# Loading the second stage's input two units at a time, with two tiles' space given up for it

## The chip, the core and the metric

The kernel runs on one core of a Trainium2 chip. The core has five engines that the text names as the profile does: PE (TensorE, matmuls; PEld is its weight load), DVE (VectorE), ACT (ScalarE), POOL (GpSimd) and SP (SyncE, which here only issues DMAs). The DMAs run on 16 DMA engines. The metric is the device time of one execution in microseconds (us); less is better.

## What is computed

All data are float32. First a causal convolution along the sequence, written in the reference with Fourier transforms, for 8 batches of 5696 positions and 128 channels; then a soft mixture of experts over all 45568 tokens.

```python
def _attn_ref(x, h):                      # x (8, 5696, 128), h (5696, 128)
    L = 2 * S
    Yf = np.fft.rfft(x, n=L, axis=1) * np.fft.rfft(h, n=L, axis=0)[None]
    return np.fft.irfft(Yf, n=L, axis=1)[:, :S, :]

def _moe_ref(x, phi, w1, w2):             # x (45568, 128), phi (128, 32), 8 experts of 4 slots, F = 1024
    logits = x @ phi
    d = softmax(logits, axis=0)           # over tokens
    slot_input = (d.T @ x).reshape(E, S_per_e, D)
    for e in range(E):
        slot_out[e] = np.maximum(slot_input[e] @ w1[e], 0.0) @ w2[e]
    c = softmax(logits, axis=1)           # over slots
    return c @ slot_out.reshape(n_slots, D)
```

## The kernel before

The transform is split into two steps of lengths 90 and 64, made of matmuls with cosine and sine tables. There are nine groups of work: group 0 is the filter h, groups 1 to 8 are the batches of x.

**First stage** (`load_x`, `fold`, `stage_a`; words `loadx`, `fold`, `low`, `high` in the order below). POOL adds and subtracts mirrored rows (line 216), PE multiplies by the first table (line 240), ACT copies the result from PSUM into a tile `fst` (line 242), and SP stores it to DRAM: `fl` for the lower half of the frequencies, `fh` for the rest (line 224 issues what was put off until the word `flush`).

**Second stage** (`load_g`, `stage_b1`, `stage_b2`; words `loadf`, `forward`, `backward`). A group has 12 units, numbered through from 0 to 107. `load_g` (line 274) brings one unit's input back from `fl` or `fh` into a tile `gt` of 4 KB in each of 128 partitions, in three buffers; the last unit of a group has 1 KB. `stage_b1` multiplies it (line 287, tile `bt`), and DVE multiplies the result by the filter's spectrum (lines 306 and 313); for group 0 DVE makes the spectrum itself (`Hr`, `Hi`, line 310). `stage_b2` transforms back (line 328, tile `bz`), ACT copies to `zst` (line 333), and after every second unit SP stores to DRAM: `zm`, or `zr` for the last rows.

**Third stage**, in 32 tiles T of 8 rows x 2 halves, four a batch. `load_main` and `load_rest` bring `zc` and `zx`; `stage_c1` (word `product`) multiplies them (lines 419 and 424) and begins to add and subtract halves into one of two tiles `y`, whose slots are addressed by `part(v, f)`; `after` (word `sums`) finishes: DVE makes the odd sum `op` and difference `om` (lines 411 and 412), POOL adds and subtracts them into y's slots (line 437). `part` transposes y (line 447), `logits` multiplies by phi into `lt`, `maximum` keeps a running column maximum, `exponents` (words `expd`, `exponent`; line 496) writes the exponentials `dt`, `stage_c5` (word `tokens`, line 505) transposes them and copies them to a tile `d` (line 508), from which `dispatch` (line 546) sums tokens into slots. Other words are the softmax over slots (`turnl`, `shift`, `exp`, `rowsum`, `scale`, `weights`).

**The order** is written out by hand: `run` takes a text of words and calls the stage that each names, with its number. Every engine carries out its instructions in this order, so a DMA whose buffer isn't free holds up all that SP is to issue after it. A loop of four passes covers batches 1 to 4 in the third stage. From `front.close()` on, the tiles of the first two stages are gone and a pool `last` stands in their place; `tail` is then filled, and `stage_c1` has DVE do part of POOL's sums. The last part is the experts and the product with `c`, line 883 and after.

Of the kernel before, what the change touches and what calls it, by code (L numbers as in the profile page):

```python
# [12 lines left out]
F32 = mybir.dt.float32  # L13
# [62 lines left out]
def kernel(  # L76
# [25 lines left out]
    P = 128  # L102
# [155 lines left out]
    def parts(u):  # L258

        g, w = divmod(u, NW)  # L260
        return g, w, [(i, min(2, NP - 2 * i)) for i in range(2 * w, min(2 * w + 2, NU))]

    def load_g(u):
        if u >= (B + 1) * NW:
            return
        g, w, us = parts(u)
        n = sum(k for _, k in us)
        t_ = bpool.tile([P, 4, 2, D], F32, name="gt", tag="gt", bufs=3)
        if 8 * w < LOW:
            src = fl[g].rearrange("h a n l o k x -> (a n l o) h (k x)")  # L270
        else:
            src = fh[g].rearrange("h a n l c o k x -> (a n l c o) h (k x)")
        k0 = 4 * w % (LOW // 2) * 2 * D
        nc.sync.dma_start(
            out=t_[:, 0:n, :, :].rearrange("p q c d -> p (q c d)"), in_=src[:, :, k0:k0 + n * 2 * D])
        gs[u] = t_
# [83 lines left out]
    om, op = [ypool.tile([P, CH, D], F32, name=n) for n in ("om", "op")]  # L360
    yt = ypool.tile([D, Q * CH, 2, MH], F32, name="yt")
    nc.vector.memset(rests[0][:, :, :, :, :], 0.0)
    for t_ in (lt, dt):
        nc.vector.memset(t_[:, :, :, :], 0.0)
    nc.vector.memset(lt[HP:P, :, :, MH - 1:MH], -2.0 ** 127)
# [35 lines left out]
    def stage_c1(T, between=lambda: None):  # L401
        zt, zx = zs.pop(T), rest.pop(T)[:, T % 2]
        y_ = ybufs.pop(0)
        ybufs.append(y_)

        def part(v, f):
            k = (2 * v + f) * CH
            return y_[:, k:k + CH, 0:D] if f == 0 else y_[:, k + CH - 1:k - 1:-1, 0:D]

        def fold_out(even, minus, plus):  # L410
            nc.vector.tensor_tensor(out=plus, in0=even, in1=minus, op=AL.add)  # L411
            nc.vector.tensor_tensor(out=minus, in0=even, in1=minus, op=AL.subtract)

        ps = {(o, c): bank() for o, c in ((0, 1), (1, 0), (0, 0), (1, 1))}
        for c in (1, 0):
            for h_ in range(2):
                for o in range(2):
                    r = slice(o * HP, (o + 1) * HP)
                    nc.tensor.matmul(ps[o, c][h_ * HP:(h_ + 1) * HP, :], im[r, c, :],  # L419
                                     zt[r, h_, :, c, :], start=True, stop=False)  # L420
        for h_ in range(2):
            for (o, c), p in ps.items():
                r = slice((2 * o + c) * HALF, (2 * o + c) * HALF + N1 - MAIN)
                nc.tensor.matmul(p[h_ * HP:(h_ + 1) * HP, :], ir[r, :], zx[r, h_, :, :],  # L424
                                 start=False, stop=True)
        ps = {k: p[:, :].rearrange("p (n d) -> p n d", d=D) for k, p in ps.items()}
        nc.scalar.activation(part(0, 0), ps[0, 1], AF.Copy)  # L427
        nc.scalar.activation(om[:, :, :], ps[1, 0], AF.Copy)
        fold_out(ps[0, 0], part(0, 0), part(1, 0))
        a_ = ps[1, 1]  # L430
        between()

        def after():
            fold_out(a_, om[:, :, :], op[:, :, :])
            for v, o_, eng in ((1, op, nc.gpsimd), (0, om, nc.vector if tail else nc.gpsimd)):
                for part_, sign in ((part(v, 1), AL.subtract), (part(v, 0), AL.add)):
                    eng.tensor_tensor(out=part_, in0=part(v, 0), in1=o_[:, :, :], op=sign)  # L437

        ys[T] = y_
        return after  # L440
# [53 lines left out]
    def exponents(T):  # L494
        for r, m in ((slice(0, P), slice(0, MH - 1)), (slice(0, HP), slice(MH - 1, MH))):
            nc.scalar.activation(dt[r, :, :, m], lt[r, :, :, m], AF.Exp,
                                 bias=low[r, T % 2:T % 2 + 1])
        if T:
            e_ = cpool.tile([P, 1], F32, name="dn", tag="dn")
            nc.scalar.activation(e_[:, :], lows.pop(T)[:, :], AF.Exp)  # L500
            scales[T] = e_
    def stage_c5(T):
# [4 lines left out]
        d_ = ypool.tile([P, CH, P], F32, name="d", tag="d", bufs=1)  # L507
        nc.scalar.activation(d_[:, :, :].rearrange("p i s -> p (i s)"), p[:, :], AF.Copy)
        ds[T] = d_
# [133 lines left out]
    def run(words, batch=0):  # L643
# [29 lines left out]
    for g in range(4):  # L673
        run(
# [54 lines left out]
    tail["last"] = last  # L729
    zring.insert(0, last.tile([P, 2, CH, 2, D], F32, name="zd"))  # L730
# [205 lines left out]
```

## Time and profile before

| | |
|---|---|
| median of 3 runs | 808.36 us (806.04 to 810.59) |
| profiled execution, own time | 805.76 us |
| profiled execution, span from first to last instruction | 803.7 us |
| mean granted TensorE clock | 0.951 |
| PE busy in the span | 712.9 us (89%) |
| DVE busy | 629.3 us (78%) |
| ACT busy | 429.3 us (53%) |
| POOL busy | 410.4 us (51%) |
| packets of SP's queue, share of 16 DMA engines' span | 96.1% |
| moved by DMA | 282.50 MB, 352 GB/s |
| loads of `gt` | 99 of 512 KB and 9 of 128 KB |

Busy time is the union of an engine's instructions. The DMA share adds up the times of packets, which can overlap, so it can be a little over 1. The span leaves out what lies before the first and after the last instruction.

### The profile page before, as it was taken

Reading aid. Unit: us, or ns where it says so; the run is one execution under the profiler, and the core shown is the slowest. Engines: PE = TensorE matmul, PEld = TensorE weight load, DVE = VectorE, ACT = ScalarE, POOL = GpSimd, SP = SyncE. Lnnn points to the kernel's source line nnn. Section 1 sums busy time; section 2 is a strip of 40 time slices with the busy share of each in tenths; the row PEclk is TensorE's granted clock in tenths of the full one; section 3 lists DMA queues with packets and bytes.
Section 4 is the critical chain, followed back from the end, with each engine's and each line's share of the span. In section 5 each row is a group of like instructions: output and inputs, shape, how many; then the busy total and the mean of one; then the engine's idle time right before and its main releaser. Section 6 shows DMA issues by size and latency. Waiting matters only on the chain.

```text
span 803.7 us, 21826 instructions
## 1 busy us (share of the span) xinstructions
PE 712.9 (89%) x8884; PEld 360.5 (45%) x8884; DVE 629.3 (78%) x895; ACT 429.3 (53%) x868; POOL 410.4 (51%) x368
## 2 busy tenths in 40 slices
PE   5768789779999999999999999999998887888882
PEld 1122233324544444554455455444444444356782
DVE  1019988648989999998999999999989996795552
ACT  2334245335666665666666566666565455474441
POOL 5545443425556666656666655566434533686000
PEclk9889999979999999999999999999999998999865
DMA  8999999999999999999999999999999899843998
GB/s 274 357 308 405 332 391 388 330 361 388 389 351 379 383 388 344 397 393 380 361 394 394 355 386 389 399 355 357 374 309 342 282 363 317 317 179 129 385 401 337
DMA packets 164779, 282.50 MB, mean 352 GB/s; under 512 B 9448, under 2 KB 128872, under 8 KB 158440
## 3 DMA queue, kind: packets, MB, share of 16 engines
q1 hardware_dynamic: 163672, 280.01, 96.1%
q8 instruction: 71, 1.16, 0.5%
q10 hardware_dynamic: 1008, 1.10, 0.4%
q14 instruction: 28, 0.23, 0.1%
HBM read 148.54 MB, written 132.53 MB: 350 GB/s over the span
## 4 chain that ended last, share of the span: by engine, by line
PE 62%; DVE 15%; DMA 14%; ACT 4%; issue 2%; POOL 1%; SPq 1%; ACTq 0%; DVEq 0%; POOLq 0%
PE bank L240 18%; PE bt L287 10%; PE bz L328 8%; PE bank L419 7%; DMA out_dram<-o 4%; PE bank L424 4%; PE bank L447 4%; DMA fl<-fst 4%; DVE yf L306 3%; DVE bt L306 3%; PE bank L456 3%; PE bank L546 2%; DVE yf L313 2%; PE bank L570 2%; DMA gt<-fh 2%
## 5 line engine op out<-in xcount | busy, mean ns | idle before, releaser
L216 POOL TENSOR_TENSOR x<-xc 128x512 f32<-128x512 f32 x144 | 179.1, 1276 | 81.5 <-PE bank L240 53.5
L240 PE MATMUL bank<-x,s 128*32 128x512 f32 x1728 | 207.1, 608 | 14.0 <-POOL x L216 8.1
L242 ACT ACTIVATE fst<-bank 128x512 f32<-128x512 f32 x216 | 125.6, 595 | 84.5 <-PE bank L240 63.3
L287 PE MATMUL bt<-gt,wt 64*64 64x256 f32 x1620 | 117.6, 399 | 26.2 <-DMA gt<-fl 9.7
L333 ACT ACTIVATE zst<-bz 128x1024 f32<-128x1024 f32 x96 | 93.0, 968 | 80.6 <-PE bz L328 74.3
L437 POOL TENSOR_TENSOR y<-y,op 128x512 f32<-128x512 f32 x64 | 78.3, 1223 | 105.2 <-DVE op L411 102.7
L306 DVE TENSOR_TENSOR yf<-bt,Hi 128x1024 f32<-128x1024 f32 x96 | 112.4, 1171 | 16.2 <-PE bt L287 16.1
L313 DVE TENSOR_TENSOR yf<-bt,yf 128x512 f32<-128x512 f32 x192 | 119.3, 663 | 3.3
L306 DVE TENSOR_TENSOR bt<-bt,Hr 128x1024 f32<-128x1024 f32 x96 | 113.0, 1177 | 0.0
L240 PEld LDWEIGHTS bank<-x,s 128*32 128x32 f32 x1728 | 52.2, 111 | 131.8 <-issue 91.8
L328 PE MATMUL bz<-yf,vt 64*64 64x256 f32 x1440 | 100.6, 387 | 4.6 <-DVE yf L313 4.2
L287 PEld LDWEIGHTS bt<-gt,wt 64*64 64x64 f32 x1620 | 54.9, 135 | 87.9 <-issue 35.6
L533 POOL TENSOR_TENSOR L<-L,rs 128x512 f32<-128x512 f32 x32 | 33.6, 1051 | 109.3 <-DVE rs L528 89.5
L328 PEld LDWEIGHTS bz<-yf,vt 64*64 64x64 f32 x1440 | 55.7, 136 | 39.8 <-DVE yf L313 11.8
L437 POOL TENSOR_TENSOR y<-y,om 128x512 f32<-128x512 f32 x54 | 64.1, 1187 | 2.1
L427 ACT ACTIVATE y<-bank 128x512 f32<-128x512 f32 x32 | 19.1, 597 | 81.6 <-PE bank L424 81.6
L447 PE MATMUL bank<-ident,y 109*128 109x109 f32 x512 | 59.4, 261 | 3.1 <-DVE y L437 1.0
L419 PE MATMUL bank<-zc,im 64*64 64x512 f32 x480 | 60.3, 600 | 0.0
L447 PEld LDWEIGHTS bank<-ident,y 109*128 109x128 f32 x512 | 49.7, 141 | 12.7 <-issue 7.9
L306 DVE TENSOR_TENSOR yf<-bt,turn 128x1024 f32<-128x1024 f32 (+1 forms) x12 | 14.0, 1170 | 52.4 <-PE bt L287 52.4
L449 ACT ACTIVATE yt<-bank 128x360 f32<-128x360 f32 x128 | 52.6, 475 | 3.7 <-PE bank L447 3.5
L883 PE MATMUL op<-so,cT 32*128 32x128 f32 x704 | 43.6, 357 | 6.5 <-ACT o L891 6.0
(99 smaller groups left out, 854.9 us busy)
## 6 DMA issues: line engine op xcount, KB each, us to landing
fl<-fst SPq DMA_DIRECT2D x72, 512.0 KB, 7.7
gt<-fl SPq DMA_DIRECT2D x72, 512.0 KB, 7.2
zm<-zst SPq DMA_DIRECT2D x64, 512.0 KB, 9.3
zc<-zm SPq DMA_DIRECT2D x30, 1024.0 KB, 9.1
fh<-fst SPq DMA_DIRECT2D x36, 512.0 KB, 6.6
xc<-in_x_dram SPq DMA_DIRECT2D x32, 512.0 KB, 8.8
out_dram<-o SPq DMA_DIRECT2D x16, 1024.0 KB, 11.2
gt<-fh SPq DMA_DIRECT2D x27, 512.0 KB, 8.2
```

Source lines behind the costliest of these rows:

```text
L216: nc.gpsimd.tensor_tensor(out=y_[:, o, :, :], in0=near, in1=far, op=AL.subtract if o else AL.add)
L240: nc.tensor.matmul(p[i * m:(i + 1) * m, :], s1[:, q + o, cols], columns(c_, o), start=True, stop=True)
L242: nc.scalar.activation(st[:, :, q, :], p[:, :].rearrange("p (n d) -> p n d", d=D), AF.Copy)
L287: nc.tensor.matmul(bt[q * HP:(q + 1) * HP, a, o, :], wt[r, 2 * i + q, :], t_[r, 2 * o + q, :, :].rearrange("p c d -> p (c d)"), start=True ...
L306: nc.vector.tensor_tensor(out=p_, in0=pv, in1=h_, op=AL.mult)
L313: nc.vector.tensor_tensor(out=y_[r, 0:k, c, :], in0=pv[:, :, c, :], in1=y_[r, 0:k, c, :], op=op_)
L328: nc.tensor.matmul(bz[a * HP:(a + 1) * HP, q, o, :], vt[r, i, a, :], y_[r, a * m + o, :, :].rearrange("p c d -> p (c d)"), start=True, sto ...
L333: nc.scalar.activation(zst[:, e_, 0:m, 0:n, :].rearrange("p o q x -> p q o x"), bz[:, 0:n, 0:m, :], AF.Copy)
L419: nc.tensor.matmul(ps[o, c][h_ * HP:(h_ + 1) * HP, :], im[r, c, :], zt[r, h_, :, c, :], start=True, stop=False)
L437: eng.tensor_tensor(out=part_, in0=part(v, 0), in1=o_[:, :, :], op=sign)
L447: nc.tensor.transpose(p[:, i * TR:(i + 1) * TR], ys[T][0:TR, k * CH + i, 0:D], ident[0:TR, 0:TR])
L449: nc.scalar.activation(yt[:, k * CH:(k + 1) * CH, :, :], of_tokens(p), AF.Copy)
```

## The change

Three edits. `load_g` now loads units u and u+1 in one DMA, into a tile of 8 KB in each partition, in two buffers; each unit gets its half, and the words `loadf` with odd numbers are taken out of the order (54 loads instead of 108; those with even numbers stay where they were, but that the first `loadf` words, 0, 1 and 2, become 0 and 2). Outside the tail the odd sum `op` has no tile of its own: it is written to y's slot `part(0, 1)`, which the last but one of POOL's four sums overwrites. `stage_c5` copies the transposed exponentials back into `dt`, from where `dispatch` reads them, instead of a tile `d`; `exponents` now runs over the whole tile in one activation, as `lt` is filled with a large negative number at the start where no token lies. In the tail, `op` and `d` are tiles of the pool `last`. The tiles given up, 4 KB in a partition, are what the larger `gt` takes.

```diff
@@ load_g
-        n = sum(k for _, k in us)
-        t_ = bpool.tile([P, 4, 2, D], F32, name="gt", tag="gt", bufs=3)
+        n = sum(k for _, k in us + parts(u + 1)[2])
+        t_ = bpool.tile([P, 8, 2, D], F32, name="gt", tag="gt", bufs=2)
...
-        gs[u] = t_
+        gs[u], gs[u + 1] = t_[:, 0:4], t_[:, 4:8]
@@ tiles of the third stage
-    om, op = [ypool.tile([P, CH, D], F32, name=n) for n in ("om", "op")]
+    om = ypool.tile([P, CH, D], F32, name="om")
...
-    for t_ in (lt, dt):
-        nc.vector.memset(t_[:, :, :, :], 0.0)
-    nc.vector.memset(lt[HP:P, :, :, MH - 1:MH], -2.0 ** 127)
+    nc.vector.memset(lt[:, :, :, :], -2.0 ** 127)
@@ stage_c1
         def after():
-            fold_out(a_, om[:, :, :], op[:, :, :])
-            for v, o_, eng in ((1, op, nc.gpsimd), (0, om, nc.vector if tail else nc.gpsimd)):
+            op = tail["op"][:, :, :] if tail else part(0, 1)
+            fold_out(a_, om[:, :, :], op)
+            for v, o_, eng in ((1, op, nc.gpsimd), (0, om[:, :, :], nc.vector if tail else nc.gpsimd)):
                 for part_, sign in ((part(v, 1), AL.subtract), (part(v, 0), AL.add)):
-                    eng.tensor_tensor(out=part_, in0=part(v, 0), in1=o_[:, :, :], op=sign)
+                    eng.tensor_tensor(out=part_, in0=part(v, 0), in1=o_, op=sign)
@@ exponents
-        for r, m in ((slice(0, P), slice(0, MH - 1)), (slice(0, HP), slice(MH - 1, MH))):
-            nc.scalar.activation(dt[r, :, :, m], lt[r, :, :, m], AF.Exp,
-                                 bias=low[r, T % 2:T % 2 + 1])
+        nc.scalar.activation(dt[:, :, :, :], lt[:, :, :, :], AF.Exp, bias=low[:, T % 2:T % 2 + 1])
@@ stage_c5
-        d_ = ypool.tile([P, CH, P], F32, name="d", tag="d", bufs=1)
-        nc.scalar.activation(d_[:, :, :].rearrange("p i s -> p (i s)"), p[:, :], AF.Copy)
-        ds[T] = d_
+        d_ = (tail.get("d") or dt)[:, :, :, :].rearrange("p i h r -> p (i h r)")
+        nc.scalar.activation(d_, p[:, :], AF.Copy)
+        ds[T] = d_.rearrange("p (i s) -> p i s", i=CH)
@@ the order, every odd loadf taken out; its first place and one of the loop
-        "loadx5 flush low7 fold8 fold9 flush high7 flush low8 loadf0 loadf1 loadf2 loadx6 flush "
+        "loadx5 flush low7 fold8 fold9 flush high7 flush low8 loadf0 loadf2 loadx6 flush "
...
-            "dispatch0 part5 part6 part7 loadf34 forward32 loadf35 flush backward31 logits1 fold32 "
+            "dispatch0 part5 part6 part7 loadf34 forward32 flush backward31 logits1 fold32 "
@@ after front.close()
+    tail["op"] = last.tile([P, CH, D], F32, name="op")
+    tail["d"] = last.tile([P, CH, 2, HP], F32, name="d")
```

68 rows, old and new, of tables (strides, w1s) are left out of this document.

## The prediction

> **What bounds the kernel now.** I read the page's engine totals, then the busy time by stage, then the chain of waits where an engine idles, then the DMA queue's own waits. By stage (PE, PEld, DVE, ACT, POOL busy with instruction counts, granted clock, DMA share, GB/s):
>
> ```profile
> 49.00:60.00 11.00, 6.93 (x64) 2.37 (x68) 3.65 (x4) 2.28 (x4) 3.36 (x4) 0.69 0.89 287
> 60.00:97.00 37.00, 29.06 (x325) 10.33 (x321) 36.25 (x42) 13.03 (x22) 19.01 (x16) 1.00 0.99 367
> 97.00:144.00 47.00, 40.42 (x510) 16.17 (x503) 39.51 (x46) 23.31 (x32) 19.62 (x16) 1.00 1.05 387
> 148.00:172.00 24.00, 15.60 (x164) 6.53 (x164) 10.95 (x12) 7.16 (x11) 4.98 (x4) 0.87 1.04 359
> 212.00:511.00 299.00, 298.69 (x3810) 148.33 (x3808) 276.63 (x385) 190.82 (x385) 187.98 (x160) 1.00 1.04 379
> 511.00:570.00 59.00, 58.93 (x738) 28.88 (x736) 54.45 (x76) 38.56 (x80) 37.49 (x32) 1.00 1.03 366
> 628.00:636.00 8.00, 6.82 (x84) 3.04 (x88) 7.79 (x15) 4.35 (x12) 1.05 (x1) 1.00 0.53 198
> 636.00:660.00 24.00, 19.81 (x264) 11.34 (x264) 22.93 (x34) 12.42 (x25) 12.53 (x11) 0.94 1.02 363
> ```
>
> From 212 to 570 us PE idles 0.4 us of 358: nothing that shortens a load, the SP queue, ACT or DVE can shorten that stretch; the change can only lengthen it. From 60 to 97 DVE is the bound (36.25 of 37). The DMA engines are as full (shares about 1): they run level with PE. Loads are on the path in three places, in the chain of waits (start, us, what):
>
> ```profile
> 42.57 6.47 DMA fl<-fst
> 49.10 3.92 DMA gt<-fl
> 53.07 1.99 PE bt L287 x16
> ...
> 144.59 4.21 DMA gt<-fl
> ...
> 159.04 7.23 DMA zr<-zst
> 166.35 5.06 DMA zx<-zr
> 171.46 2.01 PE bank L424 x16
> ...
> 636.41 7.18 DMA zm<-zst
> 644.29 12.33 DMA gt<-fh
> 656.76 1.66 PE bt L287 x16
> ```
>
> These are units 0, 24 and 106. Of other units' loads PE waits little, as issues run 10 to 18 us ahead of use (unit 36: 217.81 to 228.78; unit 38: 221.93 to 239.49) and land after a median of 7.8 us.
>
> **The change part by part.** The sum is made on the profiled execution (span 803.7, own time 805.76; the median is 808.36, 2.6 more).
>
> *The first load.* Unit 0's 4 KB rows become 8 KB rows with unit 1. Each of 16 engines moves 8 rows of the 128. The trace's packet records give a median of 159 ns for 4096 bytes and 309 for 8192, so 1.27 us becomes 2.47: forward0 starts 1.2 us later. PE runs forward0 before high9, low10 and forward1, and the DVE chain that fills 60 to 97 hangs on forward1, so all of that shifts by 1.2.
>
> *To 171 us.* From 92 to 144 the DMA engines never run dry (share 1.04), and unit 24's load waits for a store (fl of low23) behind that backlog. The start of this stretch is low15's store, 1.2 later; within it the six pairs save two packets of 159 for one of 309, 8 to an engine: about 0.07 us a pair, 0.4 in all. So loadf24 is issued 0.8 later and, being doubled, lands 2.0 later. But PE had 5.8 us of idle before L424 at 171.46, so forward24 to forward26 may all be late by 2. L424 waits for the chain zr stores, zx load. In SP's order those stores lose one load ahead of them (unit 27's, issued 155.57, 1.32 us), but its bytes are still ahead of them, now in 26's pair, and the queue is full (148 to 172: 1.04). I take 0.75 later at 171.46; bounds -1.9 (the SP time of units 25 and 27, 0.58 and 1.32, counts in full) and +2.0 (nothing absorbed).
>
> *212 to 570.* Even units' loads stand at the same places of SP's order, wait for the same forward, and carry 1.24 us more (0.5 MB at 424 GB/s, sixteen times 8192 bytes in 309 ns); odd units come earlier. The tightest is the first of a group: unit 48, issued 293.21, landed 299.26 by the trace's records, used 303.53: slack 4.3, then 3. The other tight one is zx at the turn of a batch:
>
> ```profile
> PEld bank L424 <- DMA zx<-zr: 3.3, 4, 0.9
> ```
>
> That is weight load idle (us, times, longest) in 212 to 511; PE's matmuls there still run back to back. Unit 39's load, 233.69, goes ahead of zx's, 236.97, today too, so the bytes ahead of zx don't grow. I cost this stretch at 0, bounds -0.4 (all of PE's idle) and +6 (the slower rival).
>
> *SP.* 54 fewer issues at 0.55 us, and fewer waits at L274, which hold every store behind them:
>
> ```profile
> SPq L274 <- PE bt L287: 65.3, 36, 4.3
> ```
>
> In the PE-bound stretch that is free. At the end of the loads it is not: unit 105's load is issued at 639.98 into a queue that is full until 660, while from 628 to 636 the share is 0.53. As 104's pair it goes at 629.29 into that hole, and everything behind it is served some 1.24 us earlier; 106 brings 107's 128 KB along (8 rows an engine, 5 KB for 4: 0.3). Unit 106's wait in the chain ends 0.95 earlier. Bounds 0 and -3 (of the 4.33 us that its issue took). With PE waiting 1.79 there, the next to be late is ACT's copy of the transposed exponentials, L508, 656.43 to 657.0, and dispatch25 behind it.
>
> *op and d.* The DVE sum writes y instead of op; the row that writes y already takes as long. POOL reads y where it read op (1223 ns, against 1187 for om); its idle, 132 us of the 358 from 212 to 570, hides any change: bounds -0.1 and +0.1 us each, in the tail nothing, where op has its own tile. The copy of d into dt makes the next exponents wait for dispatch: 220 against 229.9 in the first batch, ten us of room; queued behind on ACT would be zst and fst copies. If that cover went, ACT would wait out what is missing of it, once a tile. Two exponent activations become one:
>
> ```profile
> L521 ACT ACTIVATE L<-L 128x512 f32<-128x512 f32 x32 | 20.2, 632 | 49.5 <-POOL L L515 49.5
> L496 ACT ACTIVATE dt<-lt,low 128x352 f32<-128x352 f32 x32 | 18.7, 584 | 3.2 <-DVE low L470 3.1
> L496 ACT ACTIVATE dt<-lt,low 64x8 f32<-64x8 f32 x32 | 9.6, 299 | 0.0
> L411 DVE TENSOR_TENSOR op<-bank,om 128x512 f32<-128x512 f32 x32 | 21.8, 680 | 0.0
> L412 DVE TENSOR_TENSOR y<-bank,y 128x512 f32<-128x512 f32 x32 | 22.1, 691 | 1.1
> ```
>
> The pair spans 0.78 us in the timeline, one full tile 0.63: 0.15 saved, on the path two or three times after 570: -0.35. The dropped memsets (0.5 us of DVE at 3.6 us, when it idles) count nothing.
>
> Sum: +0.75 - 0.95 - 0.35 = -0.55: 805.2 for a profiled run, 807.8 as a median. A measurement of this kernel tells about 0.5% (4 us) from no change: I forecast no change.
>
> **The rivals.** *Slower, zx late.* At the turn of a batch 38's load, now 1 MB, goes ahead of the eight zr stores (223.91 to 233.6), and zx's load has to wait until they land. If the 1.24 us isn't returned by the missing load of unit 39, L424 for tiles 4, 8, 12, 16, 20 starts 1.24 late, 6.2 us in five batches. It decides as soon as zx lands over some 0.3 us later than today, as L424 at 245.71 follows L419 without a gap: 807.8 + 6.2 = 814. Against: the bytes ahead are the same.
>
> *Faster, SP was the bound.* If the stores behind L274 gain their issue times in full (-1.9 at 171 and -3 at 656, with 0.35 on ACT), with unit 0's 1.2 us hidden behind them: -5.2, 803.1. Against: in both places the DMA engines are full, and an earlier issue into a full queue lands no earlier.
>
> *Fewer DMAs, fixed cost saved.* Unit 0's load took 3.92 us for 1.27 us of packets. If the other 2.65 us used up the queue, each merged load would give it back, until PE's idle is gone: 6.6 us in 97 to 144, 8.4 in 148 to 172, about 10 in 570 to 660, and the time would be near 785. Against: with 2.65 us idle per load, shares of 1.04 could not be. The Trainium skill (DMA: Bandwidth & Descriptors, Rules for kernel authors) asks for at least 1 MiB per DMA for bandwidth, and its fit of about 2.0 us fixed plus bytes over 436 GB/s would, by an estimate, save 2 us for each of 54 loads; the trace disagrees with that as a cost of throughput, and shows it only as latency.
>
> *Nothing changes.* A pair's buffer comes free only after its second unit, and three buffers were ahead far enough: 808.4.
>
> **How the numbers follow.** Forecast 0.58 (own range 803 to 810: the bounds at 171 and 656), nothing changes 0.06, zx late 0.20, SP the bound 0.13, fixed cost 0.03. Within 0.5% (804.3 to 812.4) are the first two: 0.64. Slower 0.20, faster 0.16. The range runs from SP's case, 803.1 less half a us, to zx late, 814, and half a us: 802.5 to 814.5.
>
> **What would show it.** Right: forward0 at about 54.3, DVE's chain 1.2 late at 61.6, L424 near 172, PE idle still under 1 us between 212 and 570, forward106 about 1 us earlier against forward100, one L496 of some 630 ns a tile. Wrong: PE idle before L424 at each turn of a batch (zx late); zr stores landing 2 us sooner with the DMA share below 1 (SP the bound); a DMA share well below 1.04 in mid-kernel (fixed cost).

## The result: 0.7% slower, 812.0 us against 806.7

The changed kernel takes 811.98 us (median of 10 runs, 807.72 to 818.2), the kernel before 806.72 in the same series (804.12 to 810.59): a ratio of 1.0069, 95% interval 1.0040 to 1.0098. Two later series of the unchanged edit gave 1.0063 (1.0039 to 1.0087) and 1.0094 (1.0067 to 1.0122). The ratios and their intervals are those of the record, which leaves disturbed runs out; they are not just the quotient of two medians. The forecast of no change was wrong; the loss is that of the rival "zx late" in place and nearly in size, though its reason for the lateness did not hold as it was given.

The profiled execution took 808.70 us, with a span of 806.9 (before 805.76 and 803.7). The busy time by stage, in the stretches of the prediction (length, then PE, PEld, DVE, ACT, POOL busy with counts, granted clock, DMA share, GB/s):

```profile
49.00:60.00 11.00, 5.87 (x48) 1.79 (x48) 3.65 (x4) 2.21 (x4) 2.82 (x3) 0.69 0.90 314
148.00:172.00 24.00, 16.50 (x172) 6.21 (x164) 12.10 (x15) 8.20 (x12) 4.98 (x4) 0.93 1.02 353
212.00:511.00 299.00, 296.47 (x3776) 147.36 (x3768) 273.78 (x382) 189.86 (x367) 186.71 (x159) 1.00 1.04 377
511.00:570.00 59.00, 57.39 (x728) 27.66 (x724) 52.43 (x75) 35.31 (x69) 36.43 (x32) 1.00 1.01 350
628.00:636.00 8.00, 6.87 (x108) 4.42 (x106) 7.86 (x14) 2.98 (x6) 4.06 (x4) 1.00 0.95 369
636.00:660.00 24.00, 20.17 (x280) 10.69 (x276) 23.00 (x37) 12.86 (x26) 8.73 (x8) 1.00 0.92 322
```

From 212 to 570 us PE was busy but for 0.4 us; now it idles 2.53 + 1.61 = 4.1 us. The DMA share there is nearly what it was (1.04 and 1.01; before 1.04 and 1.03), so the DMA engines did not run dry. From 628 to 636 the hole in the DMA engines' work (a share of 0.53 before) is filled, as the prediction said of unit 104's pair.

PE's waits in 212 to 570 (us in total, times, longest us), for weights and for matmuls, then SP's own at the loads:

```profile
PEld bank L422 <- DMA zx<-zr: 8.0, 5, 2.2
...
PE bank L422 <- DMA zx<-zr: 3.5, 4, 1.3
```

```profile
SPq L274 <- PE bt L287: 38.6, 12, 5.8
```

The same in the kernel before, where no matmul waits for zx:

```profile
PEld bank L424 <- DMA zx<-zr: 4.2, 5, 0.9
...
SPq L274 <- PE bt L287: 44.2, 21, 3.6
```

L422 is the line that was L424, the matmuls that read zx. The weight loads' idle was there before without stopping PE; that PE's own matmuls now wait, four times, is the loss. SP waits for buffers 12 times instead of 21 in that window (38.6 us, 44.2 before), and up to 5.8 us at once instead of 3.6.

The chain of waits (start, us, what) at the places that the prediction showed, with the turn of the second batch added:

```profile
48.89 5.19 DMA gt<-fl
54.09 0.04 issue
54.13 1.98 PE bt L287 x16
...
146.42 5.47 DMA gt<-fl
...
159.74 8.74 DMA zr<-zst
...
168.56 4.46 DMA zx<-zr
173.02 0.04 issue
173.06 1.97 PE bank L422 x16
...
236.79 3.76 DMA zr<-zst
...
240.63 7.12 DMA zx<-zr
247.75 0.04 issue
247.80 1.12 PE bank L422 x16
...
644.33 10.85 DMA zx<-zr
655.18 0.04 issue
655.22 1.19 PE bank L422 x16
```

The same turn in the chain of the kernel before:

```profile
243.90 1.88 PE bank L419 x16
245.78 1.04 PE bank L424 x16
```

At 240.63 a DMA stands in the chain where all was PE before: by the chain, zr's stores and zx's load now set when PE goes on. At the end, unit 106's load has left the chain, and the zx load of tile 26 has taken its place.

The groups of the edited tiles (line, engine, shapes, count, then busy us, mean ns, idle before):

```profile
L494 ACT ACTIVATE dt<-lt,low 128x512 f32<-128x512 f32 x32 | 22.9, 716 | 3.3 <-DVE low L469 3.2
L409 DVE TENSOR_TENSOR y<-bank,om 128x512 f32<-128x512 f32 x27 | 18.4, 681 | 0.0
L436 POOL TENSOR_TENSOR y<-y 128x512 f32<-128x512 f32 x54 | 64.4, 1193 | 105.6 <-DVE y L409 103.5
```

The sum that now goes into y takes what it took into op (681 ns, 680 before), and POOL, which now reads y where it read op, takes 1193 ns (1223 before, a mean that includes ten sums of the tail). The one exponential takes 716 ns, not 630.

### The profile page after: what moved, and what is told of

Its sections match the earlier page's. It is cut to its first block, busy times and chain, and to the rows that moved or that the text cites. A ratio compares the mean times of both kernels' runs of the same rounds, so it can differ in the third digit from the quotient of the medians.

```text
span 806.9 us, 21715 instructions
## 1 busy us (share of the span) xinstructions
PE 711.8 (88%) x8884; PEld 360.4 (45%) x8884; DVE 628.6 (78%) x893; ACT 428.4 (53%) x836; POOL 411.5 (51%) x368
## 4 chain that ended last, share of the span: by engine, by line
PE 50%; DMA 26%; DVE 13%; ACT 4%; SPq 2%; issue 2%; POOL 1%; DVEq 0%; ACTq 0%; POOLq 0%
PE bank L240 16%; PE bt L287 8%; DMA zx<-zr 7%; PE bz L328 6%; DMA fl<-fst 5%; DMA zr<-zst 5%; PE bank L417 4%; DMA out_dram<-o 4%; PE bank L422 4%; DVE yf L306 3%; DVE bt L306 3%; PE bank L446 3%; DMA gt<-fl 2%; SPq L224 2%; DVE yf L313 2%
## 5 line engine op out<-in xcount | busy, mean ns | idle before, releaser
L287 PE MATMUL bt<-gt,wt 64*64 64x256 f32 x1620 | 115.6, 393 | 30.2 <-DMA gt<-fl 14.3
L436 POOL TENSOR_TENSOR y<-y 128x512 f32<-128x512 f32 x54 | 64.4, 1193 | 105.6 <-DVE y L409 103.5
L328 PEld LDWEIGHTS bz<-yf,vt 64*64 64x64 f32 x1440 | 53.9, 133 | 40.6 <-DVE yf L313 13.2
L436 POOL TENSOR_TENSOR y<-y,om 128x512 f32<-128x512 f32 x54 | 64.1, 1186 | 4.2
L882 PE MATMUL op<-so,cT 32*128 32x128 f32 x704 | 46.1, 376 | 4.8 <-ACT o L890 3.9
```

Of the source, the lines that this page charges most:

```text
L287: nc.tensor.matmul(bt[q * HP:(q + 1) * HP, a, o, :], wt[r, 2 * i + q, :], t_[r, 2 * o + q, :, :].rearrange("p c d -> p (c d)"), start=True ...
L328: nc.tensor.matmul(bz[a * HP:(a + 1) * HP, q, o, :], vt[r, i, a, :], y_[r, a * m + o, :, :].rearrange("p c d -> p (c d)"), start=True, sto ...
L436: eng.tensor_tensor(out=part_, in0=part(v, 0), in1=o_, op=sign)
```

## The experiments

Ratios are to runs of the kernel before on the same chip, of 5 rounds each, with the 95% interval. Two figures are worked out from each profile. The **turn delay** is the sum, over the five batch turns (tiles 4, 8, 12, 16, 20), of how much later than 24.47 us after the group's last forward (units 35, 47, 59, 71, 83) the first zx matmul starts; 24.47 is what the work between them takes when nothing waits. The **steady stretch** is from forward35's start to forward90's. "Served" is when the packets, counted in the queue's order by bytes, reach the end of a transfer: an estimate from the packet records.

### Is it the tiles, the number of buffers, or the order?

**tiles_only**: the kernel before with the edits of op, d and exponents alone; loads and order are those of before.

> The kernel before with the edits to op, d and the exponents alone; loads and their order as before. Theory 'zx late' (unit 39's half, loaded ahead of the eight zr stores at the turn of a batch, delays them and with them the load of zx; some 0.9 us of PE idle in five batches, and 1.1 us at unit 0): the time of before, -1 to +0.5 us, and no PE idle ahead of the zx matmuls at tiles 4, 8, 12, 16 and 20. Rival 'tiles' (the odd sum in y or the exponentials in dt make an engine wait): +3 to +5 us. Rival 'form' (one DMA of 8 KB rows is itself worse for the queue than two of 4 KB rows): the time of before.

805.54 us, 1.0000 (0.9975 to 1.0026). Within 0.26% the tile edits cost and bring nothing. Its profile, of an execution of 808.2 us, is not what was expected: with the old loads, PE's matmuls wait for zx three times there, 2.1 us in all.

**four_old**: tiles_only with four buffers, which the tiles given up make room for.

```diff
-        t_ = bpool.tile([P, 4, 2, D], F32, name="gt", tag="gt", bufs=3)
+        t_ = bpool.tile([P, 4, 2, D], F32, name="gt", tag="gt", bufs=4)
```

> As the kernel after in its tiles, but units loaded singly (512 KB, 4 KB rows) into four buffers of 4 KB, in the order of before. 'zx late': within 1 us of before, since no load goes ahead of the zr stores that didn't before; unit 0 on time. 'tiles': +3 to +5. 'form': the time of before.

804.21 us, 0.9987 (0.9961 to 1.0012).

**four_adj**: four_old with the changed kernel's order: the odd unit's load right behind the even one's.

```diff
-loadf36 forward34 ... part11 loadf37 forward35 loadf38 flush ... forward36 flush loadf39 loadz4
+loadf36 loadf37 forward34 ... part11 forward35 loadf38 loadf39 flush ... forward36 flush loadz4
```

> Four buffers of 4 KB as in four_old, but each odd unit's load put right behind the even one's, the order of the kernel after: the same bytes ahead of the zr stores, in DMAs of 512 KB. 'zx late': slower than before by 3 to 5 us, PE idle of about 1 us ahead of the zx matmuls at the turns of batches as in the kernel after; only unit 0's 1.1 us are gone. 'form': the time of before. 'tiles': +3 to +5, with the idle elsewhere than ahead of the zx matmuls.

805.05 us, 0.9978 (0.9953 to 1.0003), and again, as a control of a later series, 806.87 us, 1.0002 (0.9975 to 1.0029):

> four_adj again, on this chip, beside four_swap: four buffers of one unit, one 512 KB load each, the odd unit's load right behind the even one's. All theories: 0.996-1.000, at most one wait for zx of under 1 us in the five turns.

PE's waits for zx, 212 to 580 us, in the first of the two:

```profile
PEld bank L422 <- DMA zx<-zr: 0.8, 1, 0.8
```

This kernel has units 36 to 39, 2 MB, ahead of the eight zr stores just as the changed kernel has, and its matmuls never wait for zx, in either profile. (Its weight loads do: once for 0.8 us in the first, four times for 3.3 us in the second, which is more than was expected and less than the 4.2 us of the kernel before.) So having them there does not by itself make zx late, which was the rival's reason.

**move38**: the changed kernel, with the pair 38/39 (and its like of every group) loaded behind the zr stores, where unit 39's load stood.

```diff
-forward35 loadf38 flush ... forward36 flush loadz4
+forward35 flush ... forward36 flush loadf38 loadz4
```

> The kernel after with one pair's load in each batch (units 38 and 39, 50 and 51, 62 and 63, 74 and 75, 86 and 87) moved behind the zr stores, to where the odd unit's load stood before. 'zx late': the PE idle ahead of the zx matmuls at the turns of batches goes; about +1 us against before from unit 0, or up to +3 if unit 38's load now lands after its use. 'form' and 'tiles': as the kernel after, +5.

811.67 us, 1.0055 (1.0025 to 1.0084), with a turn delay of 4.9 us. It does not help: the same 1 MB is then ahead of zx's load anyway. The reading "too much ahead of the zr stores" fell here too.

### One transfer of 1 MB, or the buffer that comes free late?

These four shared one chip. **after_again** is the changed kernel.

> The kernel after, unchanged, beside the other three. Both theories: about 5 us slower than before, PE idle ahead of the zx matmuls at most turns of batches.

811.33 us, 1.0063 (1.0039 to 1.0087).

**two_dmas**: the changed kernel's pair buffers, filled by two DMAs of 512 KB in rows of 4 KB.

```diff
-        nc.sync.dma_start(
-            out=t_[:, 0:n, :, :].rearrange("p q c d -> p (q c d)"), in_=src[:, :, k0:k0 + n * 2 * D])
+        cuts = (0, 4, n) if True else (0, n)
+        for q0, q1 in zip(cuts, cuts[1:]):
+            nc.sync.dma_start(
+                out=t_[:, q0:q1, :, :].rearrange("p q c d -> p (q c d)"),
+                in_=src[:, :, k0 + q0 * 2 * D:k0 + q1 * 2 * D])
```

> The kernel after, with each pair's tile filled by two DMAs of 512 KB (4 KB rows) issued one right behind the other, instead of one DMA of 1 MB (8 KB rows); buffers, order and waits for free buffers as after. 'Form' (one DMA of 8 KB rows is served more slowly: in the kernel after 3.1 to 3.4 us for the pair 38 and 39 behind the pair before it, in four_adj 1.3 us for each single load): the time of four_adj, 0.996 to 1.000 of before. 'Release' (a pair's buffer is free only after its second unit, so unit 38's half is asked for some 2.7 us later than in four_adj, 0.7 us after forward35 starts and not 2 to 3 us before it, and the zr stores and zx come that much later): as the kernel after, 1.005 to 1.008, with the PE idle ahead of the zx matmuls.

807.34 us, 1.0014 (0.9994 to 1.0034): 0.5% better than the changed kernel beside it, and the intervals don't meet. It lies between what the two theories gave, 0.996 to 1.000 and 1.005 to 1.008. Repeated later (**two_dmas2**): 807.98 us, 1.0010 (0.9983 to 1.0037).

> The changed kernel with each pair filled by two 512 KB transfers in rows of 4 KB, again, on this chip, beside two_8k. 'Row' and 'one transfer': 1.000-1.003. If it comes at 1.005 or more, the first run of it misled, and neither the row length nor the transfer's size is the cause.

PE's waits for zx are fewer than in the changed kernel, but not gone as in four_adj:

```profile
PEld bank L425 <- DMA zx<-zr: 6.0, 5, 1.5
PE bank L425 <- DMA zx<-zr: 1.5, 3, 0.6
```

**split_turn** cuts only the first two pairs of each group of twelve units (`cuts = (0, 4, n) if w < 4 else (0, n)`), among them those at the turn; **split_rest** only the others (`w >= 4`).

> As two_dmas for the first two pairs of each group alone (units 36 to 39, 48 to 51 and so on, those loaded around the turn of a batch), one DMA for the other pairs. 'Form': 0 to +1.5 us against before, zx idle gone. 'Release': as the kernel after, +5.

> The reverse: one DMA for the first two pairs of a group, two for the others. 'Form': +3 to +5 us, since the loads at the turn are the slow ones. 'Release': +5.

809.54 us, 1.0043 (1.0016 to 1.0071), and 810.05 us, 1.0054 (1.0022 to 1.0086). Both lie between two_dmas and the changed kernel, and their intervals meet those of both, so these two runs don't tell which pairs cost. In its profile split_turn has a turn delay of 2.1 us, like two_dmas, though its time is nearer to the changed kernel's. split_rest has the turn's own pairs whole, and the worst waits of these four (in an execution of 816.7 us, well above its median):

```profile
PEld bank L425 <- DMA zx<-zr: 11.5, 5, 3.6
...
PE bank L425 <- DMA zx<-zr: 7.1, 5, 2.7
```

**four_swap**: four_adj with `loadf39 loadf38` at the turn, meant to make unit 38's load wait for forward35 as a pair's does.

> four_adj with one edit: in the pair of units that is loaded at a batch's turn (38 and 39 of every group of ten) the two 512 KB loads change places, so that the request of unit 38, which is behind unit 39's on SP's queue, also waits until forward35 has freed the buffer of unit 39. Sizes, row lengths and buffers stay those of four_adj. Theory 'release' (the pair's first half comes late because the buffer of its second half is freed last): TensorE waits for zx again at the five batch turns, as in the kernel with two 512 KB loads into one pair buffer (1 to 2 us over the five turns), and the ratio to the kernel before rises from 0.998 to 1.000-1.003. Theory 'form' (only the single transfer of 1 MB in rows of 8 KB costs): as four_adj, under 0.8 us of waits for zx, 0.996-1.000.

804.09 us, 0.9979 (0.9953 to 1.0006), turn delay 0.0. (A group has twelve units, not the ten of this text.) It is no test of the late buffer, though: buffers go round in the order of the requests, so unit 39 took the one that forward34 frees and only unit 38 waited. As much was asked for early as in four_adj.

### The length of a row, or the size of one transfer?

**two_8k**: a pair in two DMAs of 512 KB, cut by partitions (rows 0 to 63 and 64 to 127), so that rows keep 8 KB.

```diff
+        for a in range(2):
+            nc.sync.dma_start(
+                out=t_[a * HP:(a + 1) * HP, 0:n, :, :].rearrange("p q c d -> p (q c d)"),
+                in_=src[a * (src.shape[0] // 2):(a + 1) * (src.shape[0] // 2), :, k0:k0 + n * 2 * D])
```

> The changed kernel with each pair's load cut in two by partitions: two transfers of 512 KB, rows 0 to 63 and rows 64 to 127, each row still 8 KB long; buffers, release and order as in the changed kernel. Theory 'row' (the 8 KB rows are what is served more slowly): as the changed kernel, 1.005-1.007, with 7 to 11 us of waits for zx at the five turns and packets of 8 KB at 370 to 390 ns. Theory 'one transfer' (it is the size of one request, which blocks SP's queue or is done all at once): as with two 512 KB transfers of 4 KB rows, 1.000-1.003, with 2 to 6 us of waits.

877.48 us, 1.088 (1.084 to 1.092). Both theories missed by 70 us, so it tells nothing of the two. Its loads of `gt` are slow to land (KB each, median us from issue to landing):

```profile
gt<-fl SPq DMA_DIRECT2D x72, 512.0 KB, 9.6
```

In two_dmas the same 72 transfers to all 128 partitions take 6.9 us; but the 36 of 512 KB in split_rest, to 128 partitions too, also have a median of 9.6, so the landing time alone doesn't explain the loss. **one_4k** and **one_8k** put the question without that: one DMA of 1 MB each, into a tile whose halves lie 16 bytes apart (packets of 4 KB) or not (8 KB).

```diff
-        t_ = bpool.tile([P, 8, 2, D], F32, name="gt", tag="gt", bufs=2)
+        t_ = bpool.tile([P, 2, 8 * D + 4], F32, name="gt", tag="gt", bufs=2)
...
+                out=t_[:, :, 0:8 * D],
+                in_=src[:, k0:k0 + 16 * D].rearrange("r (b x) -> r b x", b=2))
```

This is one_4k; one_8k has `8 * D + 0` and fills the tile in one piece.

> The changed kernel with each 1 MB pair still loaded by one transfer, but into a tile whose two halves are 16 bytes apart in a partition, so that a packet holds 4 KB and not 8. To keep that one transfer in three dimensions its rows are taken in another order (so rows come to other partitions than in the reference, and the numbers put out aren't the reference's; the last, shorter pair of a group goes in two transfers). Theory 'row' (8 KB packets cost): as with two 512 KB transfers, 1.000-1.003, 1 to 3 us of TensorE's delay over the five batch turns. Theory 'one transfer' (its size costs, whatever the rows): as the changed kernel, 1.004-1.008, 3.5 to 5 us.

> The control of one_4k: the same order of rows and the same two transfers for a group's last pair, but no gap in the tile, so that packets hold 8 KB as in the changed kernel (rows come to other partitions than in the reference here too). Both theories: as the changed kernel, 1.004-1.008. If it comes under 1.003, the order of the rows or the two transfers of the last pair matter, and one_4k is to be read against this run and not against the changed kernel.

808.91 us, 1.0042 (1.0018 to 1.0067), and 808.32 us, 1.0033 (1.0005 to 1.0061). Packets of 4 KB do no better than packets of 8 KB, so the length of a row is not the cause of the loss. By time both come out between two_dmas and the changed kernel, and by turn delay (2.85 and 2.07 us) they are near two_dmas. 45 of their 54 pairs are one transfer, the last pair of each group two, and their rows go to other partitions; so they do not show that the size of the transfer is the cause.

### Taking the wait for the zr stores away

**after_free** and, as its control, **before_free**: at the five turns zx is filled from the other zr array, written long ago. **after_third** is the changed kernel beside them.

```diff
-            in_=zr[(b + 1) % 2]...
+            in_=zr[b % 2 if j == 0 and 0 < b < 6 else (b + 1) % 2]...
```

> The changed kernel, but at the five batch turns (tiles 4, 8, 12, 16 and 20) zx is filled from the other one of the two zr arrays, which the group before has filled long ago, so that its load needn't wait for the eight zr stores of the turn (512 KB as before, at the same place in SP's queue; the values of those five tiles are those of another batch). Theory 'turn' (the merged loads cost what they delay zx by, 3.8 to 4.4 us): waits for zx under 1 us in 212 to 580, and the ratio falls from 1.006 to 1.000-1.003. Theory 'spread' (8 KB or 1 MB transfers cost all along): the ratio stays at 1.004 or more though the waits for zx are gone.

> The same edit in the kernel before, as the control: zx at the five turns from the other zr array. Its waits for zx there are 0.1 us in sum, so both theories: 0.998-1.001.

> The changed kernel again, on this chip: 1.005-1.008, with 3 to 5 us of TensorE's delay at the five turns.

812.95 us, 1.0103 (1.0069 to 1.0136), for after_free; 805.74 us, 1.0007 (0.9985 to 1.0030), for before_free; 813.54 us, 1.0094, for after_third. That would speak for "spread", had the waits gone; but the edit did not take the lateness away. The waits in after_free, 212 to 580 us:

```profile
PEld bank L422 <- DMA zx<-zr: 7.2, 5, 2.2
PE bank L422 <- DMA zx<-zr: 2.7, 3, 1.3
```

Its zx load no longer waits: it is issued 0.05 us after the end of the issue before it, where that gap is 0.17 to 0.99 us in the changed kernel. But that is 17.4 us after the last forward, in after_third 17.9, and it is served at 23.95 against 24.00. So it can't decide between the theories. What it does show: zx is late because of the bytes that are in the queue ahead of it, not because its issue waits for zr to land.

**four_old2** repeated the one version that might beat both kernels: 805.52 us, 0.9987 (0.9962 to 1.0012), as the first time. No gain over the kernel before can be told from zero. In its profile no matmul waits for zx; the weight loads do, three times, 2.4 us in all, where no wait was expected.

> four_old again, on this chip: the changed kernel's tiles, four buffers of one unit, one 512 KB load each, in the order of the kernel before. Expected from its first run (0.9987) and from its buffers being free one unit sooner: 0.996-1.000, no wait for zx at the batch turns.

### What the profiles say together

Means over the five turns, in us after the last forward's start; the bytes are those served from that start to zx's end, and the rate is these over that time:

| kernel | last load ahead of the zr stores served | zx load issued | zx served | zx used | MB | GB/s | turn delay | steady stretch |
|---|---|---|---|---|---|---|---|---|
| before | 4.8 | 16.1 | 22.9 | 24.49 | 8.08 | 352 | 0.1 | 343.6 |
| four_adj | 5.0 | 16.1 | 22.1 | 24.47 | 7.72 | 349 | 0.0 | 343.5 |
| two_dmas | 6.2 | 17.1 | 23.1 | 24.87 | 8.07 | 349 | 2.0 | 345.5 |
| two_dmas2 | 6.2 | 17.3 | 23.4 | 25.08 | 8.03 | 343 | 3.1 | 346.5 |
| one_8k | 6.3 | 17.5 | 23.6 | 24.88 | 8.06 | 342 | 2.1 | 345.5 |
| after | 6.8 | 18.3 | 24.2 | 25.36 | 8.13 | 335 | 4.4 | 347.9 |
| after_again | 6.8 | 17.9 | 23.9 | 25.23 | 8.12 | 339 | 3.8 | 347.3 |
| after_third | 6.8 | 17.9 | 24.0 | 25.42 | 8.12 | 338 | 4.7 | 348.2 |

The steady stretch is 343.5 us plus the turn delay in every row, to 0.1 us: in these eight profiles nothing else costs there, and DMA time that doesn't end at zx is free. (In others something comes to it from elsewhere: 1.6 us in one_4k and split_rest, 0.9 in move38, 0.3 in tiles_only, 25 in two_8k.)

Against four small buffers the delay has two parts. With four, the third of the turn's four loads is asked for 2.5 us before the last forward starts (1.9 in the profile of four_adj2), with pair buffers only 0.7 after it, as the pair's buffer waits for its second unit: 0.3 MB more are left to serve, and zx comes 1.0 to 1.3 us later (four_adj to the two of two_dmas; 0.5 to 0.8 from four_adj2, served at 22.6). And the same bytes as a single transfer per pair are served more slowly: 335 to 339 GB/s against 343 and 349, and zx comes another 0.5 to 1.1 us later (to the three of the changed kernel).

Against the kernel before only the second part is new. With its three buffers it too asks for unit 38's load 0.7 us after the last forward starts, and it has as much left to serve, 8.08 MB; but it serves them at 352 GB/s. The clearest comparison is from the end of the last `c_t` load ahead of the turn's loads to zx's end, which is the same 7.92 MB in every kernel. These take 22.5 us before (22.6 and 22.7 in tiles_only and before_free, with the old loads), 22.6 and 22.8 in the two profiles of four_adj, 22.7 and 23.2 in the two of two_dmas, 23.2 in one_4k and one_8k, and 23.3 to 23.6 in the three of the changed kernel. The DMA engines' time agrees: from the last forward's start to zx's end, an engine is busy 3.00 to 3.02 us for each MB that the 16 move together in the three profiles of the changed kernel, 2.98 and 2.99 in one_8k and one_4k, 2.94 and 2.96 in the two of two_dmas, 2.92 in both of four_adj, and 2.90 before.

## Why the prediction was wrong, step by step

**The first load: right.** Unit 0's load takes 5.19 us instead of 3.92, 1.27 more (1.2 was forecast), and forward0 starts 1.06 later. In the other profiles but two_8k, too, it is 4.8 to 5.3 us from this load's issue to forward0 where the first pair comes as one transfer of 1 MB, and 3.9 to 4.4 where units 0 and 1 come in transfers of 512 KB. The start of forward0 itself ranges from 51.0 to 54.3 over all profiles, so the later start alone would show little.

**To 171 us: inside its bounds in this profile.** Unit 24's load takes 1.26 us longer, as forecast, but starts 1.8 later, not 0.8. L422 is at 173.06: 1.6 late, where 0.75 was taken and +2.0 was the bound. The other two profiles of the changed kernel have it at 177.4 and 176.7, though, where the control before_free has 173.9 and four-buffer kernels 172.4 to 175.3. The start differs from run to run by as much as the effect that is looked for.

**212 to 570: the step that failed.** It was costed at 0 because "the bytes ahead of zx don't grow". They didn't: 8.08 MB before, 8.13 after. The error was to take it that equal bytes need equal time, at the rate of the packets' median (309 ns for 8192 bytes, less than two packets of 159). The runs showed that they were served at 335 GB/s in place of 352 (339 and 338 in the other two profiles); a pair's 1 MB, asked for 0.7 us after the forward, was served 6.1 us later. zx was served 1.3 us later in a stretch where the prediction itself had found that 0.3 us decides. The term should have been +4.3 by this profile (a turn delay of 4.4 against 0.1 before; 3.8 and 4.7 in the other two). The time of a packet alone doesn't tell the late kernel: around the turns 8 KB packets took 377 to 383 ns in the changed kernel and 319 before, but 365 in four_adj and 377 in two_dmas too. That the kernel before stood at this edge shows in its own sort: the profile of tiles_only has a turn delay of 2.5 us and that of before_free 1.2, with the old loads.

**The rival "zx late": right as to place, 6.2 us forecast for 4.4.** Its mechanism, 1 MB of unit 38's load ahead of the zr stores, did not hold as given: four_adj has the same units there and no delay, move38 has that 1 MB behind them and a delay of 4.9, and after_free's zx doesn't wait for the stores and is late all the same. What counts is how fast the queue serves what is ahead of zx, and, against four buffers, when it was asked for. Its chance of 0.20 was too low for a point that it put 0.3 us from deciding.

**The end of the loads: right.** Forward106 starts 32.76 us after forward100, 0.76 less than before (0.95 forecast); what was late next is not ACT's copy but zx for tile 26, 655.22 in the chain.

**op, d and the exponents: no cost, as forecast, but no gain.** One activation of 716 ns replaced a pair that spanned 0.78 us: 0.06 saved a tile instead of 0.15, so the term of -0.35 is some -0.15. tiles_only measures 1.0000 for all three.

**"SP was the bound" and "fixed cost saved": refuted.** SP's 54 fewer issues brought nothing; the time came to 812.0 us, not 803 or 785, and the DMA share in mid-kernel stayed at 1.04. The Trainium skill (DMA: Bandwidth & Descriptors, Rules for kernel authors) would have 1 MiB or more in a DMA for the most bandwidth. In this kernel, whose DMA engines are full in mid-kernel (a share of 1.04), two DMAs of 512 KB are 0.5% faster than one of 1 MB on the same chip (1.0014 against 1.0063). The fit that the prediction took from that page of the Trainium skill stands there for DMAs that GpSimd issues; here SP issues them.

**What stays open.** The turns account for 3.8 to 4.7 us, less the 0.1 to 2.5 us that they cost in the three profiles with the old loads and three buffers, of a loss that is 5.1 to 7.6 by the three ratios. The rest is likely before 180 us: zx's first matmul starts at 175.7 in the mean of the three profiles of the changed kernel and at 173.2 in that of before, tiles_only and before_free. So few profiles don't settle that. Why a transfer of 1 MB is served more slowly isn't known; the row length is ruled out, by the likeness of one_4k and one_8k. That it is the size of the transfer rests on two_dmas beside after_again; split_turn, one_4k and one_8k lie between the two, so another reason for a part of it isn't excluded. That the late buffer delays zx by 0.5 to 1.3 us a turn against four buffers is read from profiles; between four_adj and two_dmas the medians (0.9978 and 1.0002, against 1.0014 and 1.0010) don't separate it from nothing. Three pair buffers, which would have tested it directly, need another 8 KB in each partition and weren't tried.

## What to carry to other kernels

Where PE and the DMA engines are both full, look for the one load whose data must make a round trip (stored, landed, loaded again) before PE's next step, and work out its slack in the trace: at 0.3 us of slack a change to the queue ahead of it has to be costed, and a cost of zero needs a reason, not an equality of bytes. The room that had come free held one more small buffer at no cost (four_old, 0.9987 twice, not to be told from no change) and two larger ones in place of three at a cost of 0.6 to 0.9%. A saving in issues or packets was worth nothing here, where what the queue delivers last was the bound.

## What was unexpected of the hardware

- The time of a packet depends on what else moves: 8192 bytes have a median of 309 ns over the whole kernel, but a mean of 377 to 383 around the batch turns of the changed kernel, and 319 there in the kernel before, which has 8 KB rows only in the loads of the third stage. two_dmas and four_adj also have them only there, and their mean at the turns is 377 and 365: it rose without any 8 KB row in the loads of `gt`.
- The time that SP spends in issuing DMAs moved rather than went away. From 212 to 570 us the gt issues fell from 39.5 us to 18.0, and the zm stores' issues rose from 42.6 to 64.1 and the zr stores' from 41.5 to 53.1; all issues together took 269.9 us before and 277.2 after, with 33 fewer of them.
- Loads cut by partitions were dear: with two DMAs of 64 partitions each in place of one of 128, the kernel became 8.8% slower (two_8k). 8 KB packets had a mean of 429 ns over that kernel, against 345 in the changed one. Why was not looked into.
